# An mLSTM cell with a mixture-of-depths layer: a new load order, and the depth layer spread over the next batch

## The chip, the cores and the metric

The kernel runs on one core of a Trainium2 chip. The metric is the device time of one execution in microseconds (us), the median of several runs. A profiled execution, taken apart from these, gives the trace. Its span runs from the first to the last instruction.

## The reference

Two stages, in fp32. Stage one is a recurrent cell over 768 steps, for 4 batches and 8 heads of 40 channels. With gates i and f per step and head:

```
m_new  = max(f + m, i);  fs = exp(f + m - m_new);  is = exp(i - m_new)
C      = fs*C + is * outer(v, k);   n = fs*n + is*k
y      = sigmoid(o) * (C q) / max(|n.q|, 1)
```

The outputs of the heads are joined to x of shape (4, 768, 320). Stage two picks, in each batch, the 128 rows of x with the highest scores:

```
scores = x . w_gate
top    = the 128 highest scores of the 768 rows of the batch
out    = x;   out[top] = x[top] + sigmoid(scores[top]) * (relu(x[top] @ w1) @ w2)
```

w1 is 320 x 1024 and w2 is 1024 x 320. A batch's rows can be ranked only when all of its 768 scores are known, so stage two of a batch depends on the whole of stage one of that batch.

## The kernel before, in words

**Chunks.** The 768 steps of a batch are cut into six chunks of 128 (L). Within a chunk the recurrence is written as matmuls, and only the state C (40 x 41 per head, n included) goes from chunk to chunk. There are 24 steps (b, c), in order of batch and chunk.

**Gates first.** For all batches and heads at once (32 partitions) the kernel scans the gates, chunk by chunk (L138 to L155): running sums F, running maxima Mg, the factors r and wk. Row c of Mg is stored to DRAM as M_d[c] (L150, issued by SP, the queue that issues most loads), because the chunks need it broadcast over 128 partitions. a, wk and r go through PE transposes into cols[c].

**One chunk** (`mlstm_chunk`, L169). SP loads Mb, the broadcast of M_d[c] for the batch's eight heads (L173), and GpSimd (POOL) masks it (L174). ScalarE (ACT) makes eight W = exp(...) from it (L178). TensorE (PE) transposes k and q (L185, copied by ACT at L186), forms pS = k q (L195), and VectorE (DVE) multiplies P = pS * W (L197). pI = C q from the state (L204), pC for the new state (L218, C updated by DVE at L226 and L228), pH = P v (L233). DVE adds both, makes the denominator, POOL multiplies the output gate by its reciprocal (sor, L245), DVE forms x (L246) and the score sc of each row (L249). POOL issues two stores of x, to a scratch x_d and to out (L252).

**Loads.** `load_chunk` brings k, q and v of a chunk into one of four buffers (NB), which POOL has cleared at the start: the eight heads have 40 channels in 64 columns, and the rest must be zero (for v, one). The loop calls it for up to two chunks ahead (AHEAD). `open_batch` loads the whole output gate of a batch (six loads, L334), applies one sigmoid to it (L335), clears C and takes x and sc. Exponential and sigmoid lie in different tables of ACT, so each change between them is an ACT_TABLE_LOAD. `load_weights` (w_gate, w1 and w2, issued by POOL) is called at the first step, ahead of the first chunk's code.

**Depths** (`depths`, L254), called after the last chunk of a batch. PE transposes the six columns of scores into rows (pb, L261), ACT copies them in two pieces (sb, L262), and DVE compares each column with all rows up to its own (ge, L270, 128 to 768 columns wide). 21 small matmuls add up the columns (pcol, L276), which gives each row's rank; `sel` marks the rows of rank below 128, six matmuls turn it into indices (pidx, L289), and POOL issues a gather of these rows (xe, L295). Then come the gate g, a transpose (pX, L308), the first layer as 48 matmuls (ph, L318) with relu on ACT, the second as 16 (py, L324), ye on DVE (L326) and a scatter to out issued by POOL (L327). The PSUM tiles of all of this share one pool of two buffers, ps_m.

**What sets the order.** The kernel is written in program order, and a scheduler makes each engine's instruction order from it at build time, by what is ready in its own reckoning and, among ready instructions, by program order. On the chip each engine then runs its own list strictly in order, as does SP's queue.

Of the kernel before, what the change touches and what calls it, by code (L numbers as in the profile page):

```python
# [9 lines left out]
FP = mybir.dt.float32  # L10
BF = mybir.dt.bfloat16
# [3 lines left out]
AF = mybir.ActivationFunctionType  # L15
OP = mybir.AluOpType
# [11 lines left out]
def kernel(  # L28
# [20 lines left out]
    nc = tc.nc  # L49
# [14 lines left out]
    NB = 4  # L64
    HALVES = [slice(0, 64), slice(64, 128)]
# [10 lines left out]
    outp = ctx.enter_context(tc.tile_pool(name="outp", bufs=3))  # L76
# [44 lines left out]
    xe_t = [const.tile([128, NDC * 128], FP, name=f"xe{n}") for n in range(2)]  # L121
    for n in range(2):
        nc.gpsimd.memset(xe_t[n], 0.0)
# [14 lines left out]
    for c in range(NT):  # L138
# [11 lines left out]
        nc.sync.dma_start(out=M_d[c], in_=Mg[:, c, :])  # L150
# [18 lines left out]
    def mlstm_chunk(b, c, qk, v1, C, so, x, sc):  # L169
# [84 lines left out]
    def depths(b, x, sc):  # L254

        sb = mod.tile([128, NT, L], FP, name="sb")
        for t0 in range(0, NT, 4):
            n = min(4, NT - t0)
            pb = ps_m.tile([128, n, L], FP, name="pb", tag="m")
            for t in range(n):  # L260
                nc.tensor.transpose(pb[:, t, :], sc[:, t0 + t:t0 + t + 1].to_broadcast([128, L]), ident)  # L261
            nc.scalar.copy(out=sb[:, t0:t0 + n, :], in_=pb)  # L262
# [3 lines left out]
        ge = mod.tile([128, NT, NT * L], BF, name="ge", bufs=1)  # L266
        cnt = mod.tile([128, NT], FP, name="cnt")
        for u in reversed(range(NT)):
            n = (u + 1) * L
            nc.vector.scalar_tensor_tensor(out=ge[:, u, 0:n], in0=sb.rearrange("p t l -> p (t l)")[:, 0:n],  # L270
                                           scalar=sc[:, u:u + 1], in1=earlier[:, NT * L - n:],
                                           op0=OP.is_ge, op1=OP.mult, accum_out=cnt[:, u:u + 1])
        pcol = ps_m.tile([128, NT], FP, name="pcol", tag="m")
        for t in reversed(range(NT)):
            for u in reversed(range(t, NT)):
                nc.tensor.matmul(pcol[:, t:t + 1], ge[:, u, t * L:(t + 1) * L], ones_b, start=(u == NT - 1),  # L276
                                 stop=(u == t))
# [3 lines left out]

        for j0, w in SLOTS:
# [38 lines left out]

            py = ps_m.tile([w, DM], FP, name="py", tag="m")
# [7 lines left out]

    def open_batch(b):
        so = ob.tile([128, NT, H, D], FP, name="so")
        for c in range(NT):
            nc.sync.dma_start(out=so[:, c], in_=o_gate[b, :, c * L:(c + 1) * L, :].rearrange("h p d -> p h d"))  # L334
        nc.scalar.activation(out=so, in_=so, func=AF.Sigmoid)  # L335
# [4 lines left out]
        return C, so, x, sc  # L340
# [41 lines left out]
```

## Time and profile before

| | |
|---|---|
| median of 3 runs | 277.78 us (277.69 to 279.12) |
| profiled execution | 275.82 us |
| its span | 274.1 us, 6273 instructions |
| PE busy | 196.6 us (72%) |
| DVE busy | 153.0 us (56%) |
| ACT busy | 115.8 us (42%) |
| POOL busy | 108.5 us (40%) |
| mean granted clock of TensorE | 0.841 of full |
| moved by DMA | 41.08 MB, mean 150 GB/s |

Busy time is the union of an engine's instructions; PE's weight loads are a row of their own in the profile (PEld). A share of busy time is an average over stages with different limits. The profile gives the granted clock as a share of 2.4 GHz; 0.5 of it is 1.2 GHz.

### The profile page before, as it was taken

What the parts mean: (1) busy time and instruction counts of PE and PEld (TensorE: products, weight loads), DVE (VectorE), ACT (ScalarE), POOL (GpSimd) and SP (SyncE); (2) the same over time, 40 slices, a digit from 0 to 9 for tenths busy, and PEclk for the clock granted to TensorE, in tenths of its full rate; (3) what the DMA queues carried; (4) which work ended last, traced back from release to release, by engine and by line L of the source; (5) the groups of instructions that cost most, each with busy time, mean ns of one, the idle gap of its engine ahead of it and who ended that gap; (6) DMA issues with size and microseconds to landing.
All of it is one profiled execution on the core that took longest, in us unless ns stands there. A gap on an engine that the chain in (4) does not pass through costs nothing.

```text
span 274.1 us, 6273 instructions
## 1 busy us (share of the span) xinstructions
PE 196.6 (72%) x2402; PEld 164.5 (60%) x2402; DVE 153.0 (56%) x443; ACT 115.8 (42%) x285; POOL 108.5 (40%) x155
## 2 busy tenths in 40 slices
PE   0463089987837999878798997777699998612980
PEld 0442068975626888766677976656488786501860
DVE  5800026597966407878768523897877088873100
ACT  2531486337287653636654181553543325100000
POOL 9900155167264203565454314545463055221001
PEclk9995555599995599999799999797869999965696
DMA  8799997599998633999999709597725041210000
GB/s 119 86 347 183 209 220 196 105 244 188 230 254 241 114 80 82 220 225 246 199 229 190 170 0 215 163 195 223 198 65 134 26 144 57 86 60 24 2 0 24
DMA packets 107086, 41.08 MB, mean 150 GB/s; under 512 B 101328, under 2 KB 101520, under 8 KB 107056
## 3 DMA queue, kind: packets, MB, share of 16 engines
q1 hardware_dynamic: 103680, 28.71, 54.3%
q0 software_dynamic: 3376, 11.96, 13.1%
q8 instruction: 19, 0.31, 0.6%
q14 instruction: 11, 0.09, 0.1%
HBM read 32.05 MB, written 8.62 MB: 148 GB/s over the span
## 4 chain that ended last, share of the span: by engine, by line
PE 31%; DVE 24%; issue 15%; DMA 12%; POOL 7%; SPq 6%; ACT 3%; POOLq 1%; DVEq 0%; ACTq 0%
PE ph L318 6%; PE pS L195 6%; DMA Mb<-M_d 6%; PE pH L233 5%; PE py L324 5%; DVE P L197 4%; DVE C L226 3%; POOL sor L245 3%; PE pI L204 3%; DVE ge L270 3%; SPq L98 2%; PE pt L185 2%; DVE x L246 2%; DVE C L228 2%; SPq L334 2%
## 5 line engine op out<-in xcount | busy, mean ns | idle before, releaser
L178 ACT ACTIVATE W<-Mb,cols 128x128 f32<-128x128 f32 x192 | 59.9, 391 | 34.5 <-POOL Mb L174 19.5
L233 PE MATMUL pH<-v,P 128*64 128x64 f32 x768 | 35.8, 249 | 19.0 <-DVE num L207 11.2
L186 ACT COPY qkT<-pt 128x512 f32<-128x512 f32 x48 | 26.9, 582 | 51.8 <-PE pt L185 51.3
L233 PEld LDWEIGHTS pH<-v,P 128*64 128x64 f32 x768 | 30.3, 157 | 26.7 <-DVE num L207 13.3
L185 PE MATMUL pt<-ident,qk 128*128 128x128 f32 x192 | 35.4, 318 | 15.1 <-ACT so L335 8.4
L195 PE MATMUL pS<-qkT 64*128 64x128 f32 x384 | 39.3, 324 | 1.7 <-ACT qkT L186 1.6
L174 POOL TENSOR_SCALAR_AFFINE_SELECT Mb<-Mb 128x1024 f32<-128x1024 f32 x24 | 26.7, 1116 | 31.3 <-DMA Mb<-M_d 31.3
L185 PEld LDWEIGHTS pt<-ident,qk 128*128 128x128 f32 x192 | 23.8, 158 | 19.6 <-ACT so L335 8.8
L195 PEld LDWEIGHTS pS<-qkT 64*128 64x128 f32 x384 | 31.4, 216 | 6.6 <-ACT qkT L186 3.2
L245 POOL TENSOR_TENSOR sor<-so,rec 128x320 f32<-128x320 f32 x24 | 17.4, 726 | 43.2 <-DVE rec L243 38.0
L197 DVE TENSOR_TENSOR P<-pS,W 128x512 f32<-128x512 f32 x48 | 31.9, 681 | 4.3 <-PE pS L195 3.6
L204 PE MATMUL pI<-C,qkT 128*64 128x128 f32 x320 | 25.9, 301 | 0.7 <-DVE C L228 0.7
L318 PE MATMUL ph<-xeT,w 128*128 128x128 f32 x192 | 25.3, 298 | 0.6 <-DVE g L303 0.6
L318 PEld LDWEIGHTS ph<-xeT,w 128*128 128x128 f32 x192 | 24.6, 212 | 1.6 <-DVE g L303 1.0
L246 DVE TENSOR_TENSOR x<-num,sor 128x320 f32<-128x320 f32 x20 | 12.1, 604 | 19.5 <-POOL sor L245 19.5
L212 POOL TENSOR_TENSOR wv<-v,cols 128x328 f32<-128x328 f32 x20 | 15.1, 755 | 19.1 <-PE pC L218 10.9
L204 PEld LDWEIGHTS pI<-C,qkT 128*64 128x64 f32 x320 | 19.9, 149 | 4.0 <-issue 1.1
L252 POOL DMA_DIRECT2D x_d<-x x24 | 14.0, 582 | 19.2 <-DVE x L246 18.6
L326 DVE SCALAR_TENSOR_TENSOR ye<-py,g,xe 128x320 f32<-128x320 f32 x4 | 2.2, 551 | 34.4 <-PE py L324 34.4
L270 DVE SCALAR_TENSOR_TENSOR ge<-sb,sc,earlier 128x512 bf16<-128x512 f32 (+5 forms) x24 | 16.9, 720 | 3.2 <-ACT sb L262 3.2
L226 DVE TENSOR_TENSOR C<-C,Mb 40x164 f32<-40x164 f32 x32 | 18.3, 571 | 0.5
L324 PE MATMUL py<-w,hT 128*128 128x320 f32 x64 | 17.9, 432 | 0.0
(83 smaller groups left out, 233.2 us busy)
## 6 DMA issues: line engine op xcount, KB each, us to landing
Mb<-M_d SPq DMA_DIRECT2D x24, 516.0 KB, 5.1
qk<-in_k_dram SPq DMA_DIRECT2D x24, 160.0 KB, 4.2
qk<-in_q_dram SPq DMA_DIRECT2D x24, 160.0 KB, 4.7
v<-in_v_dram SPq DMA_DIRECT2D x24, 160.0 KB, 4.2
so<-in_o_gate_dram SPq DMA_DIRECT2D x24, 160.0 KB, 4.2
x_d<-x POOLq DMA_DIRECT2D x24, 160.0 KB, 3.4
out_dram<-x POOLq DMA_DIRECT2D x24, 160.0 KB, 4.0
w<-in_moe_w_dram POOLq DMA_DIRECT2D x1, 1280.0 KB, 10.2
```

What stands on the lines that cost most here:

```text
L174: nc.gpsimd.affine_select(out=Mb[:, :, 0:L], in_=Mb[:, :, 0:L], compare_op=OP.is_ge, fill=BIG, base=0, pattern=[[0, H], [1, L]], channel_m ...
L178: nc.scalar.activation(out=W[:, h // 2, h % 2, :], in_=Mb[:, h, 0:L], func=AF.Exp, bias=cols[c][:, 0, b * H + h:b * H + h + 1], scale=-1.0)
L185: nc.tensor.transpose(pt[:, p, :], qk[:, j, 2 * p:2 * p + 2, :].rearrange("s a d -> s (a d)"), ident)
L186: nc.scalar.copy(out=qkT[:, j], in_=pt)
L195: nc.tensor.matmul(pS[j][:, p, :], qkT[e, 0, p, :], qkT[e, 1, p, :], start=True, stop=True)
L197: nc.vector.tensor_tensor(out=P[:, :, j, :], in0=pS[j], in1=W[:, :, j, :], op=OP.mult)
L204: nc.tensor.matmul(pI[t, 2 * p:2 * p + 2, :].rearrange("t a d -> t (a d)"), qkT[:, 1, p, t], C[:, p].rearrange("e a d -> e (a d)"), start= ...
L226: nc.vector.tensor_tensor(out=Cj, in0=Cj, op=OP.mult, in1=decay[e, :, j, L:L + 1].to_broadcast([D, NP, D1]))
L233: nc.tensor.matmul(pH[t, h, :], P[:, h // 2, h % 2, t], v1[:, h, :], start=True, stop=True)
L245: nc.gpsimd.tensor_tensor(out=sor, in0=so[:, c], in1=rec.unsqueeze(2).to_broadcast([128, H, D]), op=OP.mult)
L318: nc.tensor.matmul(ph[:, f, :], w1[:, j, (f0 + f) * 128:(f0 + f + 1) * 128], xeT[:, j, :], start=(j == 0), stop=(j == NDC - 1))
L324: nc.tensor.matmul(py, hT[:, f, :], w2[:, f, :], start=(f == 0), stop=(f == NFC - 1))
```

## The change

**Start.** POOL clears only the columns that no load writes. `load_chunk` now also takes Mb and loads it (four buffers instead of three, so up to two chunks ahead), behind the chunk's v. The stores of M_d are issued by ACT. The output gate of batch 0 is loaded chunk by chunk, those of chunks 0 and 1 right behind each of these chunks' loads, and its sigmoid is cut in two (chunks 0 and 1, chunks 2 to 5). w_gate is loaded on its own, ahead of everything in the loop; w1 and w2 are loaded in the second step.

**Batches.** `open_batch` of the next batch, with its six gate loads and the sigmoid, comes at chunk 3 of the batch before.

**Depths**, cut into five functions. `compare` transposes one column of scores, copies it and compares it, for the chunk before, after each chunk's code. `ranks` comes at chunk 1 of the next batch, `gather` at chunk 2, `layer1` and `layer2` at chunk 4. The layers of batch 2 do not come in batch 3: they stand at the end of the program, `layer1` ahead of the ranks of batch 3 and `layer2` behind them. `ge` is packed (2688 columns instead of 6 x 768) and has two buffers instead of one; ye has two instead of three. The work inside the functions is unchanged.

```diff
-        nc.gpsimd.memset(qk_t[n], 0.0)
-        nc.gpsimd.memset(v_t[n], 1.0)
+        nc.gpsimd.memset(qk_t[n][:, :, :, D:DP], 0.0)
+        nc.gpsimd.memset(v_t[n][:, :, D:DP], 1.0)
...
         nc.sync.dma_start(out=v_t[n][:, :, 0:D], in_=v[b, :, t, :].rearrange("h p d -> p h d"))
-        return qk_t[n], v_t[n]
+        Mb = work.tile([128, H, L + 1], FP, name="Mb", bufs=NB)
+        nc.sync.dma_start(out=Mb, in_=_bcast(M_d[c][b * H:(b + 1) * H, :], 128))
+        return qk_t[n], v_t[n], Mb
...
-        nc.sync.dma_start(out=M_d[c], in_=Mg[:, c, :])
+        nc.scalar.dma_start(out=M_d[c], in_=Mg[:, c, :])
...
+    nc.gpsimd.dma_start(out=wg, in_=_bcast(moe_w_gate, 128))
+
     def load_weights():
-        nc.gpsimd.dma_start(out=wg, in_=_bcast(moe_w_gate, 128))
...
-        Mb = work.tile([128, H, L + 1], FP, name="Mb")
-        nc.sync.dma_start(out=Mb, in_=_bcast(M_d[c][hs, :], 128))
...
+    def compare(b, u, sc, sb, ge, cnt):
+        pb = ps_m.tile([128, L], FP, name="pb", tag="m")
+        nc.tensor.transpose(pb, sc[:, u:u + 1].to_broadcast([128, L]), ident)
+        nc.scalar.copy(out=sb[:, u, :], in_=pb)
+        n = (u + 1) * L
+        nc.vector.scalar_tensor_tensor(out=ge[:, GE[u]:GE[u + 1]], in0=sb.rearrange("p t l -> p (t l)")[:, 0:n],
+                                       scalar=sc[:, u:u + 1], in1=earlier[:, NT * L - n:],
+                                       op0=OP.is_ge, op1=OP.mult, accum_out=cnt[:, u:u + 1])
...
+    def load_gates(b, so, c):
+        nc.sync.dma_start(out=so[:, c], in_=o_gate[b, :, c * L:(c + 1) * L, :].rearrange("h p d -> p h d"))
...
+    def sigmoid(so, c0, c1):
+        nc.scalar.activation(out=so[:, c0:c1], in_=so[:, c0:c1], func=AF.Sigmoid)
...
-    loaded = {}
+    loaded, state = {}, {0: open_batch(0)}
+    EARLY = 2
     for n, (b, c) in enumerate(steps):
         for step in steps[n:n + AHEAD + 1]:
             if step not in loaded:
                 loaded[step] = load_chunk(*step)
-        if c == 0:
-            state = open_batch(b)
+                if step[0] == 0 and step[1] < EARLY:
+                    load_gates(0, state[0][0][1], step[1])
+                    if step[1] == EARLY - 1:
+                        sigmoid(state[0][0][1], 0, EARLY)
         if n == 0:
+            for g in range(EARLY, NT):
+                load_gates(0, state[0][0][1], g)
+            sigmoid(state[0][0][1], EARLY, NT)
+        if n == 1:
             load_weights()
-        mlstm_chunk(b, c, *loaded[b, c], *state)
-        if c == NT - 1:
-            depths(b, *state[2:])
+        if c == NT // 2 and b + 1 < B:
+            state[b + 1] = open_batch(b + 1)
+            for g in range(NT):
+                load_gates(b + 1, state[b + 1][0][1], g)
+            sigmoid(state[b + 1][0][1], 0, NT)
+        mlstm_chunk(b, c, *loaded[b, c], *state[b][0])
+        if n > 0:
+            compare(*steps[n - 1], *state[steps[n - 1][0]][1])
+        if b > 0:
+            if c == 1:
+                todo = ranks(b - 1, *state[b - 1][1][2:])
+            elif c == 2:
+                todo = gather(b - 1, todo)
+            elif c == NT // 2 + 1 and b < B - 1:
+                layer2(b - 1, layer1(b - 1, todo))
+    compare(*steps[-1], *state[B - 1][1])
+    before_last = layer1(B - 2, todo) if B > 1 else []
+    sels = ranks(B - 1, *state[B - 1][1][2:])
+    layer2(B - 2, before_last)
+    layer2(B - 1, layer1(B - 1, gather(B - 1, sels)))
```

## Rows read from the trace of the kernel before

**Rows 1.** Windows from x to x: length, engines' busy us (instructions), PEclk, DMA share, GB/s.
```profile
0.00:45.24 45.24, 19.21 (x138) 15.69 (x140) 12.93 (x57) 20.15 (x45) 19.46 (x36) 0.72 1.03 195
45.24:79.73 34.49, 27.59 (x413) 23.06 (x409) 26.45 (x75) 16.91 (x39) 17.84 (x25) 0.88 0.91 200
79.73:139.02 59.29, 49.55 (x624) 41.45 (x624) 36.70 (x102) 33.99 (x89) 26.35 (x34) 0.86 0.81 178
139.02:194.64 55.62, 44.91 (x586) 37.76 (x585) 36.62 (x98) 25.54 (x63) 23.75 (x31) 0.94 0.78 172
194.64:243.74 49.10, 40.92 (x551) 34.63 (x551) 34.66 (x97) 17.47 (x48) 17.90 (x25) 0.91 0.32 92
243.74:274.10 30.36, 14.47 (x95) 11.95 (x95) 5.67 (x17) 1.77 (x4) 3.21 (x4) 0.67 0.07 22
```

**Rows 2.** Timeline of SP's queue at the start (start, length, line, transfer, count).
```profile
4.64 0.94 SPq L98 DMA_DIRECT2D qk<-in_q_dram  x1
8.60 3.07 SPq L150 DMA_DIRECT2D M_d<-Mg  x6
...
12.83 5.96 SPq L98 DMA_DIRECT2D qk<-in_q_dram  x1
...
21.94 6.29 SPq L334 DMA_DIRECT2D so<-in_o_gate_dram  x6
28.27 0.84 SPq L173 DMA_DIRECT2D Mb<-M_d  x1
```

**Rows 3.** Timeline of the other engines at the start.
```profile
8.45 0.12 DVE L148 COPY Mg<-r 32x1 f32<-32x1 f32 x1
...
11.00 1.61 POOL L166 DMA_DIRECT2D w<-in_moe_w_dram  x3
...
31.36 1.28 ACT L335 ACT_TABLE_LOAD   x1 [4.61 <-DMA so<-in_o_gate_dram]
...
33.21 1.08 POOL L174 TENSOR_SCALAR_AFFINE_SELECT Mb<-Mb 128x1024 f32<-128x1024 f32 x1 [19.66 <-DMA Mb<-M_d]
...
35.66 0.51 POOL L337 MEMSET C<- 128x512 f32 x1
```

**Rows 4.** Timeline of the layers in batch 3 and of the tail.
```profile
208.76 5.62 PE L318 MATMUL ph<-xeT,w 128*128 128x128 f32 x48
...
214.22 4.47 PE L324 MATMUL py<-w,hT 128*128 128x320 f32 x16
...
246.19 0.88 DVE L270 SCALAR_TENSOR_TENSOR ge<-sb,sc,earlier 128x640 bf16<-128x640 f32 x1
...
254.44 7.62 PE L318 MATMUL ph<-xeT,w 128*128 128x128 f32 x48 [0.65 <-DVE g L303]
...
267.24 1.03 POOL L327 DMA_INDIRECT out_dram<-ye,idx  x1 [16.35 <-DVE ye L326]
```

**Rows 5.** Chain of waits in order of time (start, length, what).
```profile
55.89 5.07 DMA Mb<-M_d
...
137.06 5.66 DMA Mb<-M_d
```

**Rows 6.** DMA issues: transfer, count, size, median us to landing.
```profile
M_d<-Mg SPq DMA_DIRECT2D x6, 16.1 KB, 3.9
f_sb<-in_f_gate_dram SPq DMA_DIRECT2D x1, 96.0 KB, 2.2
```

**Rows 7.** Timeline of PE, two runs of pH.
```profile
173.36 1.98 PE L233 MATMUL pH<-v,P 128*64 128x64 f32 x32 [3.75 <-DVE num L207]
...
180.96 1.15 PE L233 MATMUL pH<-v,P 128*64 128x64 f32 x32 [0.58 <-DVE num L207]
```

**Rows 8.** The page's line on packets.
```profile
DMA packets 107086, 41.08 MB, mean 150 GB/s; under 512 B 101328, under 2 KB 101520, under 8 KB 107056
```

**Rows 9.** Windows of 10 us, the one with the highest rate.
```profile
120.00:130.00 10.00, 8.74 (x161) 7.76 (x162) 7.94 (x23) 5.56 (x18) 5.63 (x7) 1.00 1.02 249
```

**Rows 10.** Waits: engine, line, waited for, us in total, times, longest.
```profile
PE pb L261 <- DVE sc L249: 11.4, 5, 4.0
```

More of the change, by code (lines that the diff above doesn't have):

```diff
@@ L64 @@
     NB = 4
+    GE = [L * u * (u + 1) // 2 for u in range(NT + 1)]
     HALVES = [slice(0, 64), slice(64, 128)]
@@ L75 @@
     mod = ctx.enter_context(tc.tile_pool(name="mod", bufs=2))
-    outp = ctx.enter_context(tc.tile_pool(name="outp", bufs=3))
+    outp = ctx.enter_context(tc.tile_pool(name="outp", bufs=2))
     dram = ctx.enter_context(tc.tile_pool(name="dram", bufs=1, space=bass.MemoryType.DRAM))
@@ L120 @@
     nc.gpsimd.memset(ones_b, 1.0)
-    xe_t = [const.tile([128, NDC * 128], FP, name=f"xe{n}") for n in range(2)]
-    for n in range(2):
+    xe_t = [const.tile([128, NDC * 128], FP, name=f"xe{n}") for n in range(2 * len(SLOTS))]
+    n_xe = [0]
+    for n in range(len(xe_t)):
         nc.gpsimd.memset(xe_t[n], 0.0)
@@ L167, in load_weights, with mlstm_chunk @@
         nc.gpsimd.dma_start(out=w2, in_=moe_w2.rearrange("(f p) d -> p f d", p=128))
[L169 removed]
+    def mlstm_chunk(b, c, qk, v1, Mb, C, so, x, sc):
         hs = slice(b * H, (b + 1) * H)
         k_n, q_n = qk[:, 0], qk[:, 1]
[L172 to L173 removed]
         nc.gpsimd.affine_select(out=Mb[:, :, 0:L], in_=Mb[:, :, 0:L], compare_op=OP.is_ge, fill=BIG, base=0,
@@ L252, in mlstm_chunk, with ranks @@
             nc.gpsimd.dma_start(out=dst[c * L:(c + 1) * L, :], in_=x[:, c, :])
[L254 to L272, printed above, removed]
+    def compare(b, u, sc, sb, ge, cnt):
[6 more added lines that the diff above has]
+                                       op0=OP.is_ge, op1=OP.mult, accum_out=cnt[:, u:u + 1])
+    def ranks(b, ge, cnt):
         pcol = ps_m.tile([128, NT], FP, name="pcol", tag="m")
@@ L275, in depths @@
             for u in reversed(range(t, NT)):
-                nc.tensor.matmul(pcol[:, t:t + 1], ge[:, u, t * L:(t + 1) * L], ones_b, start=(u == NT - 1),
+                nc.tensor.matmul(pcol[:, t:t + 1], ge[:, GE[u] + t * L:GE[u] + (t + 1) * L], ones_b, start=(u == NT - 1),
                                  stop=(u == t))
@@ L280, in depths @@
         nc.vector.tensor_tensor(out=rank, in0=rank, in1=pcol, op=OP.subtract)
+        sels = []
         for j0, w in SLOTS:
@@ L286, in depths, with gather @@
                                     in1=rank.unsqueeze(2).to_broadcast([128, NT, w]), op=OP.is_equal)
+            sels.append(sel)
+        return sels
+    def gather(b, sels):
+        picks = []
+        for (j0, w), sel in zip(SLOTS, sels):
             pidx = ps_m.tile([w, 1], FP, name="pidx", tag="m")
@@ L292, in depths @@
             nc.vector.tensor_scalar(out=idx[:, 1:2], in0=pidx, scalar1=float(b * S), scalar2=None, op0=OP.add)
-            xe = xe_t[b % 2]
+            xe = xe_t[n_xe[0] % len(xe_t)]
+            n_xe[0] += 1
             nc.gpsimd.indirect_dma_start(out=xe[0:w, 0:DM], out_offset=None, in_=x_d[b],
@@ L297, in depths, with layer1 @@
                                          bounds_check=S - 1, oob_is_err=False)
+            picks.append((w, idx, xe))
+        return picks
+    def layer1(b, picks):
+        out1 = []
+        for w, idx, xe in picks:
             scr = mod.tile([w, DM], FP, name="scre", bufs=1)
@@ L320, in depths, with layer2 @@
                 nc.scalar.activation(out=hT[:, f0:f0 + n, :], in_=ph, func=AF.Relu)
+            out1.append((w, idx, xe, g, hT))
+        return out1
+    def layer2(b, out1):
+        for w, idx, xe, g, hT in out1:
             py = ps_m.tile([w, DM], FP, name="py", tag="m")
@@ L329, in depths @@
                                          in_=ye, in_offset=None, bounds_check=B * S - 1, oob_is_err=False)
+    def load_gates(b, so, c):
+        nc.sync.dma_start(out=so[:, c], in_=o_gate[b, :, c * L:(c + 1) * L, :].rearrange("h p d -> p h d"))
     def open_batch(b):
         so = ob.tile([128, NT, H, D], FP, name="so")
-        for c in range(NT):
-            nc.sync.dma_start(out=so[:, c], in_=o_gate[b, :, c * L:(c + 1) * L, :].rearrange("h p d -> p h d"))
-        nc.scalar.activation(out=so, in_=so, func=AF.Sigmoid)
         C = ob.tile([128, NP, 2, DP], FP, name="C")
@@ L339, in open_batch @@
         sc = xp.tile([128, NT], FP, name="sc")
-        return C, so, x, sc
+        sb = mod.tile([128, NT, L], FP, name="sb")
+        ge = mod.tile([128, GE[NT]], BF, name="ge")
+        cnt = mod.tile([128, NT], FP, name="cnt")
+        return (C, so, x, sc), (sc, sb, ge, cnt)
+    def sigmoid(so, c0, c1):
+        nc.scalar.activation(out=so[:, c0:c1], in_=so[:, c0:c1], func=AF.Sigmoid)
     steps = [(b, c) for b in range(B) for c in range(NT)]
-    loaded = {}
+    loaded, state = {}, {0: open_batch(0)}
+    EARLY = 2
     for n, (b, c) in enumerate(steps):
```

## The prediction

> **What bounds the kernel now.** I read the windows by batch first, then SP's queue and the timeline at the start, the timeline of the layers, and the chain of waits. No engine is the bound over the whole span: the windows show different limits in turn.
>
> From 0 to 45.24 us, where the first chunk's x ends, nothing but loading sets the time: PE is busy 19.21 of 45.24 us and the transfers move 195 GB/s [rows 1]. The reader is to see in SP's queue why: by 5.6 us it has issued the loads of chunk 0 and k and q of chunk 1, but the first chunk's Mb leaves only at 28.27, behind six M_d stores, loads of chunk 2 (one issue took 5.96 us) and six o_gate loads [rows 2]. The mask on that Mb starts at 33.21 [rows 3], and 12.0 us later x ends.
>
> The five remaining chunks of batch 0 take 34.49 us, 6.9 each. Batches 1 to 3 take 59.29, 55.62 and 49.10 us [rows 1]. Each of these holds the layers of the batch before as one block on PE: 5.62 us of L318 and 4.47 us of L324 in the last one, 10.1 together [rows 4]. And three times, once in batch 0 and twice in batch 1, the chain stands for 4.4 to 5.7 us, 15.2 in all, on an Mb that was issued when it was needed (the first and the last are shown) [rows 5].
>
> After the last x, 30.36 us remain, in which PE is busy 14.47 [rows 1]: rank, gather and layers of batch 3 in a row, with nothing beside them.
>
> **The change, part by part.** The profiled execution took 275.82 us, 1.72 more than its span of 274.10; the median of the runs is 277.78, 1.96 above it. I sum against the span and add both.
>
> One thing has to be settled first: what moving code is worth. The engines' order is not the program's: the C of batch 1 is cleared at 35.66, before the first chunk has an x [rows 3]. So a scheduler places what is ready, and program order decides only between ready instructions. A later place in the program therefore lowers a rank; it does not forbid an early place.
>
> *Start.* M_d of chunk 0 needs the copy at 8.45 [rows 3]; on ACT it leaves at about 9, between exponentials. A lone load landed in 2.2 us, the M_d stores in 3.9 [rows 6], so Mb can be issued at 11 to 13; I take 12.5, by the row of M_d itself. Ahead of it on SP are then the loads of chunks 0 and 1 and perhaps two of o_gate, most of them issued by 5.6 us. In the kernel before, Mb took 4.9 us from issue to mask (28.27 to 33.21). I add 3 us, an estimate, because the weight loads, although lower in rank, will still leave at about 11 us while POOL stands idle [rows 3], and beside them the issue in rows 2 lasted 5.96 us. Mask at 20.4, x 12.0 later: 32.4, taken as 32. That is 13.2 us gained. Bounds: 11 + 4.9 + 10 = 26, if the first chunk also has a fast clock; 41, 4 us below now, if Mb stays behind the weights and all loads of chunk 2. What waits behind Mb on SP are loads of chunks 1 and 2, not needed for another 10 us.
>
> The Trainium skill (DMA: Bandwidth & Descriptors, section "Issuing engines are not separate DMA queues") says that transfers started by different engines share the same 16 DMA engines, and that another issuer saves only issue time. By that rule M_d gains no bandwidth on ACT and lands in the row's 3.9 us; with a path of its own it would land in 2.2, and the sum would be 1.7 us less. I go by the row.
>
> *Smaller clears on POOL, the gate weights' own early load, a split sigmoid.* POOL is idle 19.66 us ahead of the first mask [rows 3], so shorter clears are worth nothing. A fifth sigmoid costs one table load there and one back, 1.28 us each [rows 3]; ACT is busy 20.15 of the first 45.24 us, so nothing, or 2.6 us if that cover is gone. Six ACT copies per batch in place of two fall on an engine busy 25.54 of 55.62 us [rows 1]: nothing.
>
> *Mb two chunks ahead, with a fourth buffer.* The three waits [rows 5] lose their cause. What is late next is DVE and PE themselves. In batch 0 I count little: after an early first chunk the next ones are fed by transfers, which moved 200 GB/s at 6.9 us a chunk [rows 1]. 34 us instead of 34.49.
>
> *Layers.* Batch 3 of the kernel before is the cleanest: 49.10 us with a block of 10.1, so 39.0 without. Its block moves behind the last chunk: 39.5, and 9.6 gained. Batches 1 and 2 keep one block each, and besides batch 3's work they have a sigmoid and full loads: 49.10 + 1.4 = 50.5 each, which gains 8.8 and 5.1. That the block comes at chunk 4 instead of 0 or 1 I count at nothing: it displaces the same PE time wherever it lies. Bounds for the two: 43 each (half or more of the layers in PE's gaps), and 59.29 and 55.62 (as now).
>
> *Tail.* Between the last x and ph at 254.44 PE has only 14.47 - 7.62 - 4.47 = 2.4 us of work in 10.7 [rows 1, 4], so there is room for most of batch 2's 10.1. One comparison of 640 columns, 0.88 us, is done earlier [rows 4]. Against that, py of batch 2, 4.47 us in one run, can stand on PE ahead of the six pidx matmuls on which the gather hangs, and its scatter, 1.03 us [rows 4], on POOL ahead of the gather: I count 3.5 us for both. Tail 30.36 - 0.9 + 3.5 = 33.0. Bounds: 27.5, if nothing stands in the way and the last ph runs in 5.62 instead of 7.62 us because PE has been busy; 40, if all of the layers come first. I don't count the clock: after 3.75 us of idling pH took 1.98 us, where another run of it took 1.15 [rows 7], and PE will idle nearly as long for the gather.
>
> Sum: 32 + 34 + 50.5 + 50.5 + 39.5 + 33.0 = 239.5 us of span, 34.6 less. With 1.72 and 1.96: 243.
>
> **Rivals.**
> *Transfers take over.* At 195 GB/s 6.2 MB are moved by 32 us, so some 34 of 41.08 MB [rows 8] remain, nearly all before the last x. At 200 GB/s (batch 0) that is 170 us and ends just before the forecast's last x, at 206.5; at the 172 of batch 2 [rows 1] it is 198, the last x comes at 230 and the end at 230 + 33 + 3.7 = 267. For it: in batch 0 transfers ran at 200 GB/s with their share at 0.91. Against it: a stretch of 10 us ran at 249 [rows 9], and the 172 includes a block in which little was asked for.
> The Trainium skill (the same page, section "Specifications") asks for at least 512 B in one piece for the full rate. The trace agrees that nearly all pieces are smaller, 101328 of 107086 packets [rows 8], which speaks for a ceiling that cannot be raised here, near the row's 249.
>
> *Layers fill PE's gaps.* Ranked low, the 48 + 16 matmuls of a batch could be set singly between the chunks' own. Then batches 1 and 2 take 43: 243 - 15 = 228. For it: PE has gaps, 8 us in batch 3 and 10 in each of the others [rows 1]. Against it: each of the four L318 groups stands as one unbroken run in the trace, two of them in rows 4.
>
> *The layers of batch 2 do not move.* Their inputs are ready from chunk 2 of batch 3, and the scheduler may put them where they are now. Then batch 3 stays at 49.1 and the tail at 29.5: 243 + 9.6 - 3.5 = 249.
>
> *Slower: the transposes of the scores stall PE.* Today 24 of them come in groups before two copies a batch, and 5 waited for sc, 11.4 us in all, 2.3 each [rows 10]. The change ties one to each chunk, in the same queue as the chunk's own matmuls. If the other 19 also wait 2.3 us, that adds 43 us and gives 286. From 1.8 us each on it eats the whole gain. For it: PE's queue is in order, and sc comes at the end of a chunk's DVE chain. Against it: the comparison is written after the next chunk, so sc is older when it is wanted.
>
> **How the numbers follow.** Forecast 62%, transfers 14%, gaps 13%, not moved 5%, slower 6%. The forecast's own range, by start and tail, is 233 to 255. To hold 8 in 10 I reach past the gap case below and most of the way to the transfers above: 226 to 262. A difference of 0.5%, 1.4 us, is about what can be told from none. All cases but the last lie far below that: faster 0.91; the last, with a spread that reaches to zero, gives slower 0.06 and same 0.03.
>
> **What would show it.** Right: Mb of chunk 0 issued before 16 us and the first x ended near 32; no Mb landing of 4 us or more in the chain after the start; one L318 run in each of batches 1 and 2, none in batch 3 and two after its last x; batch 3 near 40 us, the tail near 33. Wrong: the first x after 40, chunks of batch 0 over 7.5 us with transfers busy throughout, or PE waiting for sc in most chunks.

## The result, and the profile after

The changed kernel takes 263.58 us (median of 4 runs, 263.01 to 263.96) where the kernel before took 277.82 beside it (277.69 to 279.12): ratio 0.9476, interval 0.9443 to 0.9509. The gain is 14.2 us; 34.6 were forecast, and the time lies 1.6 us above the range. The profiled execution took 263.01 us with a span of 261.3. Single runs are at times disturbed and some per cent longer; the ratios leave these out, and where too few others are left (late sigmoid, loads alone, no weights, half of Mb), the median and the range stand without one.

The windows from x to x of the changed kernel, cut as in [rows 1]: start, batches 0 to 3, tail.

```profile
0.00:26.02 26.02, 15.34 (x133) 11.78 (x133) 12.25 (x55) 13.90 (x30) 14.03 (x33) 1.00 0.99 189
26.02:79.28 53.26, 30.68 (x436) 25.99 (x434) 28.59 (x78) 32.45 (x82) 22.32 (x31) 0.78 1.03 224
79.28:130.23 50.95, 44.12 (x594) 37.61 (x594) 36.00 (x100) 28.79 (x75) 26.69 (x34) 0.93 0.91 205
130.23:179.15 48.92, 42.47 (x594) 36.21 (x594) 35.09 (x100) 28.13 (x72) 23.49 (x31) 0.97 0.82 191
179.15:218.20 39.05, 30.00 (x485) 25.64 (x485) 31.06 (x96) 14.02 (x40) 14.80 (x22) 0.88 0.35 92
218.20:261.30 43.10, 27.29 (x162) 23.40 (x162) 5.69 (x17) 2.86 (x6) 4.22 (x5) 0.78 0.06 20
```

Against the forecast's 32, 34, 50.5, 50.5, 39.5 and 33.0 the reader is to see two terms far off, batch 0 (19.3 us longer) and the tail (10.1 longer), and the start 6.0 shorter. Batches 1 to 3 are within 1.6 us. The start's gain of 19.2 us is gone when batch 0 ends: 79.28 us, where the kernel before stood at 79.73 [rows 1].

**Batch 0.** The first x ends at 26.02, the second at 48.69; what lies between is in the timeline of all engines (start, length, engine, line, what; in brackets the idle time before it and who ended it):

```profile
12.31 0.61 POOL L171 DMA_DIRECT2D w<-in_moe_w_dram  x1
12.49 0.82 SPq L102 DMA_DIRECT2D Mb<-M_d  x2
...
17.56 1.09 POOL L177 TENSOR_SCALAR_AFFINE_SELECT Mb<-Mb 128x1024 f32<-128x1024 f32 x1 [4.63 <-DMA Mb<-M_d]
18.60 1.11 POOL L171 DMA_DIRECT2D w<-in_moe_w_dram  x2
...
19.68 0.96 POOL L172 DMA_DIRECT2D w<-in_moe_w_dram  x1
...
20.59 12.19 SPq L350 DMA_DIRECT2D so<-in_o_gate_dram  x4
...
22.14 0.69 ACT L181 ACTIVATE W<-Mb,cols 128x128 f32<-128x128 f32 x2
25.53 0.49 DVE L249 TENSOR_TENSOR x<-pH,sor 128x320 f32<-128x320 f32 x1 [0.91 <-POOL sor L248]
...
36.26 1.28 ACT L364 ACT_TABLE_LOAD   x1 [13.42 <-DMA so<-in_o_gate_dram]
37.55 1.27 ACT L364 ACTIVATE so<-so 128x1280 f32<-128x1280 f32 x1
...
40.12 1.86 ACT L181 ACTIVATE W<-Mb,cols 128x128 f32<-128x128 f32 x6
...
41.72 1.29 DVE L200 TENSOR_TENSOR P<-pS,W 128x512 f32<-128x512 f32 x2 [13.44 <-ACT W L181]
...
42.56 2.27 PE L236 MATMUL pH<-v,P 128*64 128x64 f32 x32 [14.85 <-DVE P L200]
```

Read from below: PE waits 14.85 us for P, DVE 13.44 for the last six of chunk 1's eight exponentials. ACT has done two of them at 22.14 and then stands 13.42 us in front of the second sigmoid, which the scheduler put between them; the other six start at 40.12, behind it. That sigmoid waits for gates 2 to 5. Their four loads, 160 KB each, take SP 12.19 us merely to issue, where the first four of such loads, at 1.72 to 4.43, took 2.6 together. In front of them, at 12.31, 18.60 and 19.68, POOL has sent off w1 and w2, 2.62 MB.

One line of the transfer view over each kernel's time up to the end of batch 0 shows that this was no single accident. Before, 0 to 79.7 us:

```profile
DMA packets 46327, 15.73 MB, mean 197 GB/s; under 512 B 44160, under 2 KB 44352, under 8 KB 46319
```

After, 0 to 79.3 us:

```profile
DMA packets 46630, 16.84 MB, mean 212 GB/s; under 512 B 44192, under 2 KB 44384, under 8 KB 46623
```

Both kernels end batch 0 at the same time with nearly the same transfers done, in both with the transfer engines' share near 1. That alone does not show that batch 0 could not end sooner, since SP's queue also loads ahead for batch 1; what the loads cost is tested in runs six to eleven.

The mean rate is no measure of it. To end batch 0 at the forecast 66 us with 16.84 MB moved would have asked for 255 GB/s, and the kernel before went faster than that for a while: 249 is not its highest rate over 10 us, as the heading of [rows 9] has it. Its page gives the rate in 40 slices of 6.85 us:

```profile
GB/s 119 86 347 183 209 220 196 105 244 188 230 254 241 114 80 82 220 225 246 199 229 190 170 0 215 163 195 223 198 65 134 26 144 57 86 60 24 2 0 24
```

The third slice, with the weights under way, has 347, and from 13 to 23 us the mean is 306. So the ceiling near 249 that the prediction read from that row does not hold: the rate depends on which loads are under way, and run seven puts a price on the two kinds.

**The tail.** PE's timeline in the changed kernel, from the last comparison on:

```profile
218.88 0.44 PE L262 MATMUL pb<-ident,sc 128*128 128x128 f32 x1 [3.82 <-DVE sc L252]
...
221.30 7.76 PE L331 MATMUL ph<-xeT,w 128*128 128x128 f32 x48 [1.34 <-DVE rank L277]
228.90 0.67 PE L274 MATMUL pcol<-ones_b,ge 128*128 128x1 bf16 x21
229.82 4.57 PE L342 MATMUL py<-w,hT 128*128 128x320 f32 x16 [0.25 <-DVE rank L278]
234.23 0.29 PE L294 MATMUL pidx<-token,sel 128*128 128x1 f16 x6
...
241.22 8.05 PE L331 MATMUL ph<-xeT,w 128*128 128x128 f32 x48 [0.65 <-DVE xeT L323]
```

POOL's timeline there, a scatter of batch 2 and the gather of batch 3:

```profile
235.27 1.02 POOL L345 DMA_INDIRECT out_dram<-ye,idx  x1 [15.65 <-DVE idx L297]
236.59 1.07 POOL L301 DMA_INDIRECT xe<-x_d,idx  x1 [0.30 <-issue]
```

The same steps in the kernel before:

```profile
247.14 0.67 PE L276 MATMUL pcol<-ones_b,ge 128*128 128x1 bf16 x19 [0.59 <-DVE ge L270]
249.05 0.32 PE L289 MATMUL pidx<-token,sel 128*128 128x1 f16 x6 [1.25 <-DVE sel L285]
249.84 1.06 POOL L295 DMA_INDIRECT xe<-x_d,idx  x1 [4.68 <-DVE idx L292]
```

The 48 matmuls of batch 2's first layer stand ahead of pcol, on which the rank of batch 3 hangs, the 16 of its second layer ahead of pidx, on which the gather hangs, and a scatter ahead of the gather. Batch 3's own first layer starts 23.0 us after the last x (241.22 less 218.20); before, it was 10.7 (254.44 less 243.74, [rows 1, 4]). Step by step, the way from the last x to pcol is 7.3 us longer, from pcol to pidx 3.4, from pidx to the gather 1.6, and from the gather on the same: 12.3 in all.

### The profile page after: what moved, and what is told of

It reads as the page before. It is cut to its first block, busy times and chain, and to the rows that moved or that the text cites. A ratio compares the mean times of both kernels' runs of the same rounds, so it can differ in the third digit from the quotient of the medians.

```text
span 261.3 us, 6263 instructions
## 1 busy us (share of the span) xinstructions
PE 189.9 (73%) x2402; PEld 160.6 (61%) x2402; DVE 148.7 (57%) x443; ACT 120.1 (46%) x304; POOL 105.5 (40%) x155
## 2 busy tenths in 40 slices
DMA packets 107085, 41.07 MB, mean 157 GB/s; under 512 B 101328, under 2 KB 101520, under 8 KB 107056
## 3 DMA queue, kind: packets, MB, share of 16 engines
q1 hardware_dynamic: 103392, 28.61, 55.8%
## 4 chain that ended last, share of the span: by engine, by line
issue 23%; DMA 20%; DVE 19%; PE 12%; SPq 10%; POOL 10%; ACT 2%; POOLq 1%; ACTq 0%; DVEq 0%
DMA Mb<-M_d 10%; POOL sor L248 5%; SPq L350 5%; PE pH L236 3%; DVE P L200 3%; DVE x L249 3%; SPq L100 3%; DMA out_dram<-x 3%; PE ph L331 2%; DMA qk<-in_k_dram 2%; SPq L99 2%; DVE ge L265 2%; POOL Mb L177 2%; DMA so<-in_o_gate_dram 2%; DVE C L229 2%
## 5 line engine op out<-in xcount | busy, mean ns | idle before, releaser
L181 ACT ACTIVATE W<-Mb,cols 128x128 f32<-128x128 f32 x192 | 61.2, 392 | 22.8 <-POOL Mb L177 11.8
L236 PE MATMUL pH<-v,P 128*64 128x64 f32 x768 | 30.9, 232 | 24.9 <-DVE P L200 19.7
L236 PEld LDWEIGHTS pH<-v,P 128*64 128x64 f32 x768 | 26.5, 144 | 30.9 <-issue 15.4
L200 DVE TENSOR_TENSOR P<-pS,W 128x512 f32<-128x512 f32 x48 | 31.9, 680 | 17.0 <-ACT W L181 16.6
L198 PE MATMUL pS<-qkT 64*128 64x128 f32 x384 | 35.6, 319 | 3.0 <-ACT qkT L189 3.0
L198 PEld LDWEIGHTS pS<-qkT 64*128 64x128 f32 x384 | 29.3, 216 | 7.9 <-ACT qkT L189 4.2
L189 ACT COPY qkT<-pt 128x512 f32<-128x512 f32 x48 | 26.9, 581 | 14.3 <-PE pt L188 14.2
L331 PE MATMUL ph<-xeT,w 128*128 128x128 f32 x192 | 27.1, 311 | 3.0 <-DVE xeT L323 1.6
L331 PEld LDWEIGHTS ph<-xeT,w 128*128 128x128 f32 x192 | 26.3, 225 | 4.1 <-DVE xeT L323 2.2
L249 DVE TENSOR_TENSOR x<-num,sor 128x320 f32<-128x320 f32 x20 | 11.4, 570 | 18.9 <-POOL sor L248 18.9
L265 DVE SCALAR_TENSOR_TENSOR ge<-sb,sc,earlier 128x128 bf16<-128x128 f32 (+5 forms) x24 | 19.9, 830 | 2.9 <-ACT sb L263 2.4
L262 PE MATMUL pb<-ident,sc 128*128 128x128 f32 x24 | 8.5, 356 | 15.8 <-DVE sc L252 15.8
L263 ACT COPY sb<-pb 128x128 f32<-128x128 f32 x24 | 6.2, 260 | 28.5 <-PE pb L262 28.5
```

The costliest lines, as they stand in the source:

```text
L181: nc.scalar.activation(out=W[:, h // 2, h % 2, :], in_=Mb[:, h, 0:L], func=AF.Exp, bias=cols[c][:, 0, b * H + h:b * H + h + 1], scale=-1.0)
L189: nc.scalar.copy(out=qkT[:, j], in_=pt)
L198: nc.tensor.matmul(pS[j][:, p, :], qkT[e, 0, p, :], qkT[e, 1, p, :], start=True, stop=True)
L200: nc.vector.tensor_tensor(out=P[:, :, j, :], in0=pS[j], in1=W[:, :, j, :], op=OP.mult)
L236: nc.tensor.matmul(pH[t, h, :], P[:, h // 2, h % 2, t], v1[:, h, :], start=True, stop=True)
L249: nc.vector.tensor_tensor(out=x[:, c, :].rearrange("p (h d) -> p h d", d=D), in0=num[:, :, 0:D], in1=sor, op=OP.mult)
```

## Experiments

The kernels ran in three groups (one to four, five to eight, nine to eleven), each beside the kernel before on the same chip; kernels of different groups are compared by their ratios to it. "Ended" is the end of the last x of a batch.

**One: the second sigmoid later.** It is written ahead of chunk 2, which needs it first, and no longer behind the gates' loads.

```diff
         if n == 0:
             for g in range(EARLY, NT):
                 load_gates(0, state[0][0][1], g)
+        if n == EARLY:
             sigmoid(state[0][0][1], EARLY, NT)
```

> The changed kernel, with the second sigmoid of batch 0 (chunks 2 to 5) called ahead of chunk 2 instead of chunk 0; its loads stay where they are. Theory A (ACT's queue): in the changed kernel this sigmoid stands between the exponentials of chunk 1 and waits 13.4 us for its loads, and chunk 1 waits behind it; x of chunk 1 then ends near 37 instead of 48.7, and the kernel takes 250 to 254 us. Rival B (transfers): the first 79 us move 16.9 MB at 213 GB/s and the best stretches run at 228, so at most 5 us can be had; the wait goes to loads of k, q, v or Mb, and the kernel takes 258 to 264.

Measured: 272.29 us (265.22 to 273.6). Its total and its later stages are not used. In its profile the second x starts at 43.11 instead of 48.20. Chunk 1 has its reciprocal at 33.95, but its `sor` stands on POOL behind chunk 3's wv, and this waits for v, which SP issued at 35.05, behind the four gate loads. In the waits from 26 to 80 us of this kernel:

```profile
POOL wv L215 <- DMA v<-in_v_dram: 8.0, 1, 8.0
```

The third x comes 11.5 us after the second. Batch 0 ended 2.7 us earlier. The theory falls: most of the lateness moved to another wait for a load that came late, on another engine's ordered list.

**Two: the layers of batch 2 back in batch 3.**

```diff
-            elif c == NT // 2 + 1 and b < B - 1:
+            elif c == NT // 2 + 1:
                 layer2(b - 1, layer1(b - 1, todo))
 ...
```

> The changed kernel, with the layers of batch 2 at chunk 4 of batch 3, as for the batches before, and not at the end. Theory A: moving them bought 9.6 us in batch 3 and cost 12.7 in the tail, where they stand as a whole ahead of the gather and mostly at half clock; so batch 3 takes 48 to 50 us, the tail 30 to 31, and the kernel 259 to 262 us, faster than the changed one. Rival B (what the prediction assumed, room in the tail): the tail grew for another reason (ranks, clock), stays near 40, and the kernel takes 268 to 273.

Measured: 260.98 us (258.94 to 262.1), ratio 0.947 (0.9352 to 0.9589). Batch 3 takes 47.9 us and the tail 29.2: together 77.1, against 82.2 in the changed kernel. The ratio does not tell this kernel from the changed one, and its batch 2 took 3.0 us longer (51.9); but within these two stages, moving the block behind the last x cost 5.0 us more than leaving it.

**Three and four: loads alone, depths alone.** The kernel before with the new start and load order only; and the changed kernel with the old load order (M_d stored on SP, Mb loaded when a chunk begins, all gates of a batch at its first chunk, one sigmoid). The edit that tells the two apart best, put in by the one and taken out by the other:

```diff
+        Mb = work.tile([128, H, L + 1], FP, name="Mb", bufs=NB)
+        nc.sync.dma_start(out=Mb, in_=_bcast(M_d[c][b * H:(b + 1) * H, :], 128))
+        return qk_t[n], v_t[n], Mb
```

> The kernel before, with the loading part of the change alone (order of the first loads, Mb with its chunk, M_d issued by ACT, smaller clears, next batch's gate at chunk 3); ranking, gather and layers as before. Theory A: the gain in batches 1 and 2 (8.3 and 6.7 us) comes from Mb loaded ahead, and the start's gain is lost to the sigmoid by the end of batch 0; so 260 to 266 us. Rival B: that gain comes from spreading the depth layer; then the loads alone give 274 to 278.

> The kernel before, with the depth part of the change alone (compare, ranks, gather and layers placed as in the changed kernel), loads as before. Theory A: nothing gained in batches 1 and 2, 9.6 gained in batch 3, 12.7 lost in the tail: 277 to 283 us. Rival B (spreading gains in batches 1 and 2): 262 to 270.

Measured: loads alone 264.82 us (259.17 to 266.58); depths alone 277.3 (271.57 to 279.58), ratio 1.0026 (0.9971 to 1.008). All four runs of the loads alone lie below all of the kernel before beside it (274.33 to 283.54); so the loads carry most of the change's gain or all of it, though no ratio says how much. The depths alone win nothing as a whole: in their profile batch 3 takes 39.5 us and the tail 42.9, which is 9.6 won and 12.5 given back against [rows 1]. That profile, at 271.57 us the shortest of the ten runs, also has batches 1 and 2 shorter by 3.9 and 3.1 us, which the median does not bear out.

**Five: the tail split.** The first layer of batch 2 goes ahead of the last two comparisons, its second layer behind the last gather.

```diff
+        if n == len(steps) - 1:
+            before_last = layer1(B - 2, todo)
         if n > 0:
             compare(*steps[n - 1], *state[steps[n - 1][0]][1])
 ...
-    before_last = layer1(B - 2, todo) if B > 1 else []
-    sels = ranks(B - 1, *state[B - 1][1][2:])
+    last = gather(B - 1, ranks(B - 1, *state[B - 1][1][2:]))
     layer2(B - 2, before_last)
-    layer2(B - 1, layer1(B - 1, gather(B - 1, sels)))
+    layer2(B - 1, layer1(B - 1, last))
```

> The changed kernel, with the first layer of batch 2 called ahead of the last two comparisons and its second layer behind the gather of batch 3. Theory A (the tail's loss is the order on PE): the first layer runs in PE's idle time before and beside the last comparison, the second in the gather's shadow; the tail falls from 43.1 to 31 to 34 us, and the kernel takes 252 to 255 us. Rival B (room in the tail is not there because the last ph needs PE warm, or the scatter of batch 2 holds POOL): the tail stays at 38 or more, the kernel at 258 to 263.

Measured: 255.87 us (254.4 to 256.79), ratio 0.9314 (0.9234 to 0.9394). PE's timeline of this kernel, whose last x ends at 219.4:

```profile
216.52 5.18 PE L331 MATMUL ph<-xeT,w 128*128 128x128 f32 x44
221.53 0.27 PE L262 MATMUL pb<-ident,sc 128*128 128x128 f32 x1
...
224.41 0.68 PE L274 MATMUL pcol<-ones_b,ge 128*128 128x1 bf16 x21 [1.70 <-DVE ge L265]
226.33 0.32 PE L294 MATMUL pidx<-token,sel 128*128 128x1 f16 x6 [1.25 <-DVE sel L284]
226.52 7.33 PE L342 MATMUL py<-w,hT 128*128 128x320 f32 x16
233.69 0.49 PE L321 MATMUL pX<-ident,xe 128*128 128x128 f32 x3
234.96 5.62 PE L331 MATMUL ph<-xeT,w 128*128 128x128 f32 x48 [0.78 <-DVE xeT L323]
```

pcol and pidx no longer stand behind a layer, py runs while the gather is under way (it outlasts it: the rows are there at 230.2, pX starts at 233.69), and the tail takes 33.2 us: the forecast's 33.0, by an order that the change did not have.

**Six: no weights.** w1 and w2 are not loaded but cleared, by DVE, so that the layers add nothing.

```diff
 ...
-        for j, (d0, w) in enumerate(HW):
-            nc.gpsimd.dma_start(out=w1[0:w, j, :], in_=moe_w1[d0:d0 + w, :])
-        nc.gpsimd.dma_start(out=w2, in_=moe_w2.rearrange("(f p) d -> p f d", p=128))
+        nc.vector.memset(w1, 0.0)
+        nc.vector.memset(w2, 0.0)
```

> The changed kernel without the loads of w1 and w2 (2.62 MB of 41.07; both are zeros, so the layers add nothing). Theory B (transfers bound all of batch 0): its last x comes 2.62 MB / 0.22 MB per us = 11.9 us earlier, at 66 to 69 instead of 79.3 us, and most of that stays: 250 to 254 us. Theory A (one wait on ACT for the gate, transfers not the bound otherwise): the gate lands earlier, the wait shrinks, but from chunk 2 to 5 nothing changes (30.6 us for four chunks); the last x of batch 0 at 71 to 75.

Measured: 257.88 us (254.6 to 266.62). The second x follows the first by 9.5 us instead of 22.7, ACT waits 0.84 us ahead of the second sigmoid, and batch 0 takes 39.45. The windows of batch 0 and batch 1 in this kernel:

```profile
31.39:70.84 39.45, 28.62 (x465) 24.27 (x463) 31.50 (x79) 28.24 (x73) 20.39 (x27) 0.96 1.06 226
70.84:121.46 50.62, 44.37 (x594) 37.60 (x594) 35.84 (x100) 27.92 (x74) 26.45 (x34) 0.93 0.87 202
```

Batch 0 ended 8.4 us earlier, and the transfer share in it is still above 1: other loads are next in line. The ends are to be compared here, not the lengths: the first x ended at 31.39 instead of 26.02, because ACT's copies of chunk 0's transposes (qkT) came behind its eight exponentials, at 22.66 instead of 15.84. The same holds for ten and eleven (31.06 and 30.26). The second x ended at 40.91 instead of 48.69.

**Seven: half of Mb.** Only four of the eight heads' masks are loaded, the rest stay constant; the number of packets is the same.

```diff
 ...
-        nc.sync.dma_start(out=Mb, in_=_bcast(M_d[c][b * H:(b + 1) * H, :], 128))
+        nc.sync.dma_start(out=Mb[:, 0:H // 2], in_=_bcast(M_d[c][b * H:b * H + H // 2, :], 128))
```

> The changed kernel with only four of eight heads of Mb loaded per chunk (the other half keeps ones; 6.3 MB of 41.07 left out, instructions otherwise the same). Theory B (transfers bound batch 0 and much of batches 1 and 2): batch 0 ends 6 x 0.264 MB / 0.22 = 7 us earlier, chunks of batch 0 from the third on take 6.3 instead of 7.65 us, batches 1 and 2 fall to 45 to 48, together 245 to 252 us. Theory A (queue order and engines bound them): batches 1 and 2 stay at 49 to 51 and the kernel at 257 to 262.

Measured: 273.95 us (268.52 to 277.22). The page's queue lines of this kernel (packets, MB, share of 16 engines' span), and under them those of the changed kernel:

```profile
DMA packets 107086, 34.74 MB, mean 128 GB/s; under 512 B 101328, under 2 KB 101520, under 8 KB 107056
...
q1 hardware_dynamic: 103392, 22.27, 47.3%
```

```profile
q1 hardware_dynamic: 103392, 28.61, 55.8%
```

6.34 MB less changed nothing for the better. ACT still waited 14.08 us for the gates, and batch 0 ended at 78.16, only 1.1 us earlier, where theory B asked for 7. So the sum of the transfers does not set that end by itself: it also depends on which loads come ahead of which. Batches 1 and 2 took 55.4 and 54.5 us, with the transfers' share at 0.68 in both; why these are slower than in the changed kernel is open. The shares give a price, an estimate: 55.8% of 16 x 261.3 us is 2333, 47.3% of 16 x 270.4 is 2046, so half of Mb took 287 us of packet time, 354 GB/s over 16 engines. What is left, less the other half's 287, is 1759 us, nearly all of it for the 15.7 MB of k, q, v and o_gate in 98304 pieces of 160 B: 143 GB/s. The rule of the Trainium skill that the prediction named (DMA: Bandwidth & Descriptors, "Specifications": small pieces fall short of the full rate) is borne out by these shares.

**Eight: the weights held.** One-element copies make the four loads wait for the score of chunk 4 of batch 0.

```diff
+        for j in range(NDC):
+            nc.vector.tensor_copy(out=w1[0:1, j, 0:1], in_=late)
+        nc.vector.tensor_copy(out=w2[0:1, 0, 0:1], in_=late)
 ...
-        if n == 1:
-            load_weights()
+        if n == 5:
+            load_weights(state[0][0][3][0:1, 4:5])
```

> The changed kernel, with w1 and w2 held back until the score of chunk 4 of batch 0 exists (four one-element copies of it into w1 and w2 ahead of their loads). Theory B, strong form (transfers bound batches 0 and 1 alike): batch 0 ends 10 to 12 us earlier, batch 1 takes as much longer, the kernel 260 to 264 us. Weak form (batch 1 has room, since PE's block falls in it): 5 to 10 us stay, 253 to 258 us. Theory A: batch 0 ends at 71 to 76 and the kernel takes 256 to 261.

Measured: 262.01 us (260.62 to 266.46), ratio 0.9514 (0.9429 to 0.96). Against the changed kernel's 0.9476 that is no difference. The time lies in the range of theory B's strong form, outside those of its weak form and of A. Its profiled run, 266.46 us, stands apart from the rest, so its stages do not decide; where the weights go is read from ten, which has the same edit.

**Nine: half of the pieces.**

```diff
-            nc.sync.dma_start(out=qk_t[n][:, j, :, 0:D], in_=src[b, :, t, :].rearrange("h p d -> p h d"))
+            nc.sync.dma_start(out=qk_t[n][:, j, 0:H // 2, 0:D], in_=src[b, 0:H // 2, t, :].rearrange("h p d -> p h d"))
```

(and v and o_gate likewise). The tiles of the other heads hold constants; for that the k, q and v tiles are now cleared whole, and by DVE instead of POOL.

> Only heads 0 to 3 of k, q, v and o_gate are loaded (half of the 160-byte pieces); the tiles' other heads hold constants. Every instruction of the engines stays as it is, so the heads 4 to 7 are computed from constants. Mb and the weights are loaded whole. From the queue shares of the changed kernel and of the run with half of Mb, a load of k, q, v or o_gate (1024 pieces) takes 1.14 us of all 16 transfer engines, one Mb 1.5 us, the weights 7.5 us; until the end of batch 0 some 36 of the 160-byte loads are made, 41 us of the 79. Theory A (until the end of batch 0 the transfers' own time is the bound, and it is mostly the pieces'): 20 us of it go, the end of batch 0 comes at 58 to 66 us instead of 79.3, and batches 1 and 2, which are bound by PE and DVE, keep 48 to 53 us each; the whole takes 243 to 252. Rival B (the order of the issues and single waits on a landing set batch 0, not the transfers' total): the end of batch 0 stays at 72 or later, the whole at 256 or more.

Measured: 270.52 us (270.24 to 272.05), ratio 0.9834 (0.9781 to 0.9888). By the numbers theory A fell: batch 0 ended at 72.6. The trace shows that the edit changed the start as well. DVE clears until 7.4 us, so its first scan of the gates starts at 7.55 instead of 3.10 and the first M_d leaves at 11.91 instead of 8.59. SP's queue in this kernel:

```profile
13.02 1.60 SPq L350 DMA_DIRECT2D so<-in_o_gate_dram  x3
14.72 8.52 SPq L102 DMA_DIRECT2D Mb<-M_d  x4
```

The first Mb now leaves behind four chunks' loads and nine gate loads, at 14.72, three more Mb right behind it. Its mask starts at 23.45, and the first x ends at 37.04, 11 us later than in the changed kernel. From there on:

```profile
37.04:72.61 35.57, 25.84 (x438) 21.79 (x439) 31.21 (x79) 22.41 (x65) 19.78 (x27) 1.00 0.61 174
72.61:131.26 58.65, 45.87 (x592) 39.12 (x590) 38.12 (x100) 27.84 (x72) 26.57 (x35) 0.88 0.49 128
```

The rest of batch 0 takes 35.57 us with the transfers at 0.61, not 53.26 at 1.03. That fits A, but neither the end of batch 0 nor the total tests it, as the start had changed too, and why batch 1 takes 58.65 here stays open.

**Ten and eleven: tail split, weights held to chunk 4 of batch 0, or to its last chunk.** The edits of five and eight; in eleven:

```diff
-        if n == 1:
-            load_weights()
+        if n == 6:
+            load_weights(state[0][0][3][0:1, 5:6])
```

> The first layer of batch 2 stands ahead of the last two comparisons, its second layer behind the last gather, and the four loads of w1 and w2 wait for the score of chunk 4 of batch 0. Each alone gave 255.87 and 262.01 against the changed kernel's 263.58. Theory A (the two edits are in different stages, and neither uses the other's room): 254.3, between 252 and 256.5, with the tail at 31 to 34 and batch 0 ended at 74 to 78. Rival B (holding the weights only moves their 7.5 us of transfers to the end of batch 0, as chunk 5 of the held run suggests, and is worth nothing): 255.5 to 258.

> As the run before, but the loads of w1 and w2 wait for the score of chunk 5 of batch 0, the last, so that they run beside batch 1, whose layers of batch 0 need them at its chunk 4. Theory A (batch 0 is bound by transfers, batch 1 by PE and DVE with room for 7.5 us of transfers beside them): batch 0 ends at 70 to 74 us as in the run without weights, batch 1 keeps 50 to 53, and the whole takes 247 to 252. Rival B (the transfers are the bound through batch 1 too): batch 0 ends earlier, batch 1 takes as much longer, 55 or more, and the whole is 254 to 258.

Measured: 249.72 us (248.66 to 253.43), ratio 0.9055 (0.8993 to 0.9117), and 250.05 (249.79 to 254.72), ratio 0.9076 (0.9024 to 0.9129). Both beat the two kernels of the case and the tail split alone. Ten is also below its expected 252, more than the two edits gave singly; why is open. Batch 0 and batch 1 of ten, where the weights are issued from 63.7 to 66.3 us:

```profile
31.06:75.49 44.43, 37.52 (x567) 32.10 (x565) 33.46 (x95) 26.82 (x68) 22.07 (x30) 0.92 1.06 244
75.49:124.50 49.01, 37.26 (x493) 31.42 (x489) 32.59 (x88) 28.00 (x75) 27.12 (x35) 0.93 0.98 222
```

and of eleven, where they are issued from 70.5 to 73.1:

```profile
30.26:67.55 37.29, 29.83 (x465) 25.73 (x463) 28.78 (x78) 24.93 (x63) 18.71 (x26) 0.91 1.12 226
67.55:125.78 58.23, 46.32 (x591) 38.87 (x589) 39.11 (x105) 30.71 (x81) 30.60 (x40) 0.91 0.96 233
```

In eleven the last x of batch 0 ends at 68.07, 0.5 us behind the cut of the windows. A's total came in, but by B's stages: batch 0 ended early, and batch 1 took some 58 us. Part of the lateness follows the weights: in ten the Mb issued right behind them, at 65.95, landed after 13.5 us, where 5.6 is the changed kernel's median. But a batch's length is not their price alone, since chunks of the two batches overlap here: in ten the first x of batch 1 ends 0.5 us after the last of batch 0, in eleven its first two end 0.4 us apart, at 81.31 and 81.71. The second x of batch 1 ends at 94.47 in the changed kernel, at 82.37 in ten, at 81.71 in eleven, and at 85.59 with no weights at all; the last at 130.23, 124.50, 125.78 and 121.46. So holding the weights back is worth 12 to 13 us at the start of batch 1, of which 4.5 to 5.7 are left at its end. Up to there the same loads in another order are worth at least as much as leaving the weights out.

## Why the prediction was wrong

**Start: 32 forecast, 26.0 measured, the lower bound.** Mb left at 12.49, as worked out (12.5). M_d, issued by ACT, landed in 3.2 us (median), nearer to the row's 3.9 than to the 2.2 of a path of its own. Neither surcharge came: the mask started 5.1 us after the issue, not 7.9 (most of the weights left only at 18.60), and x ended 8.5 us after the mask, not 12.0, at a granted clock of 1.00 where the start before had 0.72 [rows 1].

**Batch 0: 34 forecast, 53.3 measured. This step failed.** It took 6.9 us a chunk from a window in which the weights and all of batch 0's gates had already landed: before, they were loaded inside the 45.24 us of the start. The change moved the first x ahead of them, not them out of the way. The prediction saw that the weights would leave early in spite of their later place, and charged them 3 us on the first Mb; they fell on chunk 1. At the 354 GB/s of run seven their 2.62 MB are an estimated 7.4 us of all transfer engines, and the four gate loads another 4.6 by the same run's price of small pieces: 12.0 of the 13.3 us by which the end of batch 0 missed the forecast's 66. Without the weights batch 0 ends 8.4 us earlier (run six, 70.84), with the weights held back 11.2 (run eleven, 68.07). Why the second is more than the weights' own time is open.

**The split sigmoid, costed at nothing or 2.6 us for its tables.** The sum held only its work. It also puts a wait for gates 2 to 5 into ACT's ordered list between chunk 1's exponentials, and "ACT is busy 20.15 of 45.24" covers work, not what stands behind a wait. It was the place of 13.4 us; run one shows that without it 5.1 us are won at the second x and 2.7 at the end of batch 0, and the rest is spent waiting for later loads.

**Batches 1 to 3: 50.5, 50.5 and 39.5 forecast, 50.95, 48.92 and 39.05 measured.** Blocks of layers stayed blocks, one L331 run in batch 1 and one in batch 2, none in batch 3, two in the tail. That batch 1 would gain 8.8 us came out (8.3), but how much of it is due to the Mb issued early and how much to the block moved is open, as only the depths alone left a profile that can be compared (batch 1 in 55.4 us there). One sign that the prediction had named for being right did not come: landings of Mb of 4 us and more still stand in the changed kernel's chain of waits after the start.

```profile
35.89 4.51 DMA Mb<-M_d
63.42 5.54 DMA Mb<-M_d
...
146.63 6.47 DMA Mb<-M_d
156.91 5.85 DMA Mb<-M_d
...
187.67 4.04 DMA Mb<-M_d
```

Batch 1 has none of them any more, where it had two. Batch 2, between 130.23 and 179.15, has two and before had none, and yet came out 1.6 us below its forecast; there the number was right without the mechanism.

**Tail: 33.0 forecast, 43.1 measured, beyond the bound of 40. The second step that failed.** The mechanism was named: matmuls of batch 2's layers ahead of what the gather hangs on. It was mis-sized. For py and the scatter 3.5 us were put, and they cost 5.0; for the first layer nothing was put, and it cost 7.3, because it was thought to fit in PE's idle time, 10.7 us less 2.4 of work, ahead of batch 3's first layer. Those idle spells lie between steps of one chain, and a run of 48 matmuls, once started, delays the next step by its whole length. It also ran in 7.76 us and not in 5.62. Runs two and five show both the cost and the cure.

**The rivals.** "Transfers take over" was nearest (267) and got 14%. Its mechanism held in part, in the first 80 us and not over the whole span: it was argued from a mean rate, where the share of 1.03 and 0.91 up to the end of batch 0 [rows 1] already told that the transfer engines had little room there, so that a load moved forward puts another one back. The layers did not fill PE's gaps; those of batch 2 did move; and pb waited for sc 15.8 us in all, 10 times, against 11.4 in 5 [rows 10], far from the 43 us that the rival added. Two sums of the prediction do not come out, with no bearing on the miss: by its own bounds for start and tail the forecast's range is 231 to 259, not 233 to 255, and its chances for the cases that are faster add up to 0.94, not 0.91.

## What to carry to other kernels

Where transfer engines are busy from the start on, an order that brings the first result forward moves the wait to the next one, unless loads that are needed much later are held back as well, as the weights in ten and eleven. Before counting a gain, price the loads of the stage by the transfer time of their packets, not by bytes and one mean rate. Price an instruction moved into an in-order list by what it waits for, not by its length alone, and work put into an idle spell by the next step of the chain that is queued behind it. Work that is to fill a wait must be written behind the instructions that start the wait, as the second layer behind the last gather.

## What the runs showed of the hardware that had not been expected

- By run seven's shares, packets of 160 B took an estimated 17.9 ns of a transfer engine each (143 GB/s over 16), Mb's of 2 KB and more 354 GB/s. Run nine's share agrees roughly: 32.3% of 16 x 268.5 us is 1388; less 574 for a whole Mb, 814 us are left for 49152 pieces, 16.6 ns each. k, q, v and o_gate are 38% of the 41.07 MB and, by these figures, some 60% of the transfer time.
- Issuing took SP longer while the transfer engines had much in hand: 0.4 to 0.9 us for each of the first four 160 KB loads, 12.19 us for four at 20.59, behind the weights. In run eleven, with no weights ahead of them, the same four took 4.98. That SP's queue was full is inferred, not shown.
- The granted clock differed with what PE had done before. The first layer of batch 2 ran at a granted clock of 0.71 (7.76 us) after a stretch at 0.50 in which PE was busy 1.08 of 5.3 us. In run five, behind a chunk's matmuls, it had 1.00, and py, 7.33 us at 0.62 where 4.47 is usual, took the slow stretch, beside the gather, where it cost less.
